# An attention and MoE kernel on one core: value preparation placed between a batch's first scores and its first x, and the last block's last step tile by tile

## The chip, the core and the metric

The kernel runs on one core of one Trainium2 chip. A core has a matrix engine (PE, whose weight loads are listed apart as PEld), three engines for elementwise work (DVE, ACT, POOL) and SP, which here only issues DMAs. Each engine runs its own stream of instructions in order and waits for the others by semaphores. Matmuls write to PSUM, which has eight banks of 128 × 512 float32; SBUF is the working memory.

The metric is the device time of one execution in microseconds. It is told as the median of several runs; a profile shows one execution.

## The reference

Eight batches of 576 tokens and eight heads of 64 columns go through attention over pooled keys and values, and the result, as 4608 tokens of 512 columns, through a gated MLP with 2048 hidden columns.

```python
k_p = k.reshape(B, H, 72, 8, D).mean(axis=3)      # keys and values pooled by 8
v_p = v.reshape(B, H, 72, 8, D).mean(axis=3)
scores = q @ k_p.T / sqrt(D)
attn = softmax(scores)
x = attn @ v_p                                     # (4608, 512), heads side by side
h = x @ w_in
g = h * clip(h + 3, 0, 6) / 6
out = g @ w_out
```

All of it is in float32. The kernel splits an operand into a high and a low part (float32r) and adds three products, high by high, high by low and low by high.

## The kernel before

**Blocks.** The tokens are cut into ten blocks (`BLOCKS`, L22): 512, 256, 384, six of 512 and 384. For each block the MLP runs in 16 steps, one for each group of 128 hidden columns (`Step`, L761). A step makes `h` (12 matmuls at L774, into one of two PSUM banks), then `relu` on ACT (L782), `gate` on DVE (L786), `hi` on ACT (L790) and `lo` on DVE (L794). Two steps later its `out` adds three matmuls for each tile of 128 tokens (L803) into the tile's own PSUM bank. After the 16th step ACT scales the tile (L806) and SP stores it (L808).

**Attention under the MLP.** While block j runs its MLP, the attention of block j + 1 is made between its pieces. "Block j's run" below is that stretch. The attention is a list of steps (`block_steps`, L609): a scores step for a tile and half of the heads (matmuls L412, maximum on DVE L416, exponentials on ACT L420, division on POOL L448 and L454), a transposes step (L518 and L520 on PE, then L529 and L540 on ACT, L530 and L541 on DVE, which empty the PSUM bank), and an x step (`av`, L578: the products with the values at L583 and a copy by ACT at L585). `Paced` spreads the list evenly over the slots of the MLP: one in each `h`, one before each tile of an `out`. At the end of a run `split_x` (L556) makes the next block's x into its two parts.

**Side steps.** A batch's keys and values are prepared from batch 2 on by side steps (`side_steps`, L592): four loads of keys (L200) and four sums by eight on DVE (L214) with two scalings on ACT each (L222); six loads of values (L228, and L233 in three DMAs each) and six sums on DVE (L332), after the fourth and the last of which ACT and DVE write the values' parts (L345, L346, L359, L360). `plan()` (L970) attaches each side step to an attention step, which it goes ahead of. Loads, the sums of values (`vsum`), the second half of a q tile that spans two batches and the outputs share a ring of four SBUF buffers (`ring`, L131). The prepared keys and values have two buffers each, by turns of the batches.

**Order.** Up to the third step of block 1's run, the order of each engine's instructions is written out by hand (`ORDER`, L32; the numbers count an engine's instructions in program order), and `put_in_order` (L141) fixes it. Behind it the framework lays the instructions out, by program order and by what a simulated timeline finds ready.

Of the kernel before, what the change touches and what calls it, by code (L numbers as in the profile page):

```python
# [8 lines left out]
F32 = mybir.dt.float32  # L9
# [8 lines left out]
P = 128  # L18
# [3 lines left out]
BLOCKS = [512, 256, 384] + [512] * 6 + [384]  # L22
# [1 line left out]

TLAG = 3

SIDE = 20

WSCALE = 2.0**8

# [28 lines left out]
        93 62 90 85 87 94 117-120 91 126-129 99 102 92 115 103 100 112 136 65 130 137 101 138-139 116 113 124  # L59
        121 114 125 122 140 123 143 66 63 131 64 132 134 144 135 153 133 145 141 147 142 150 148 146 154 151 149  # L60
        155 157 160 156 152 166 158 161 159 167 170-172 162-163 168 164 173 165 174 176 178 169 175 183 177
        180-181 179 187 186 184 188 185 194-197 189 202-205 198-199 182 200 208-211 190-191 201 206-207 192
        212-213 193
    """,
    "Pool": """
# [1 line left out]
    """,  # L67
    "SP": """
        2-3 1 0 4-5 8 6-7 14 9 11 10 22-24 21 20 13 12 15 18 16 19 25-26 28 31 17 27 32 34 33 29 41 30 44 51 35
        48 46 43 36 47 39 52 59 42 37-38 45 40 50 49 53-55 57-58 60-62 64 63 56  # L70
    """,
}

# [2 lines left out]
def attention_moe_kernel(  # L76
# [19 lines left out]
    nc = tc.nc  # L96
    NB, _, NPAIR, S = q.shape
    SP = S // POOL
    NT, DM = out.shape
    NF = w_in.shape[0]  # L100
# [7 lines left out]
    starts = [sum(BLOCKS[:j]) for j in range(len(BLOCKS))]  # L108

    parts_of = []  # L110
    for j, t in enumerate(starts):
        end, mine = t + BLOCKS[j], []
        while t < end:
            n = min(end, (t // S + 1) * S, t + (256 if j == 0 else end)) - t
# [14 lines left out]
    psum = ctx.enter_context(tc.tile_pool(name="psum", bufs=1, space=PSUM))  # L129

    def ring(name):  # L131
        return pool.tile([P, S], F32, name=name, tag="ring", bufs=4)

    def behind(ins, name):
        no_sync = mybir.DependencyInfo(mybir.DependencyClass.NoSync, mybir.DependencyReason.DATA)
        tc.add_manual_dep(ins, name, no_sync, reason="order")

    traced = nc.cur_bb.bb.instructions
# [59 lines left out]
    def load_k(b, p):  # L198
        kraw[b, p] = ring("kst")
        nc.sync.dma_start(kraw[b, p], k[b, p])  # L200
# [3 lines left out]
    def prep_k(b, p):  # L204

        two = b == 0
        if not two:
            ks = pool.tile([P, 1, SP], F32, name="ksum", bufs=1)
        elif p % 2 == 0:
            ks = ksum[p // 2] = piece(0, 2 * SP).rearrange("p (i s) -> p i s", i=2)  # L210
        else:
            ks = ksum[p // 2]
        i = p % 2 if two else 0
        nc.vector.tensor_reduce(  # L214
            out=ks[:, i], in_=kraw.pop((b, p)).rearrange("p (s o) -> p s o", o=POOL), axis=AX.X, op=ALU.add
        )
        if i == two:

            scale = 1.0 / (POOL * D**0.5)
            for h in range(2):  # L220
                rows = slice(h * D, (h + 1) * D)
                nc.scalar.mul(kbds[b % 2][rows, p - i : p + 1, h * SP : (h + 1) * SP], ks[rows], scale)  # L222
# [3 lines left out]
    def load_v(b, p):  # L226
        vraw[b, p] = ring("vst")
        nc.sync.dma_start(vraw[b, p][:, : POOL * D], v[b, p])  # L228

    def load_vr(b, g):  # L230
        vraw[b, NPAIR + g] = ring("vst")
        for c in range(3):
            nc.sync.dma_start(vraw[b, NPAIR + g][c * REM : (c + 1) * REM, : POOL * D], vr[b, g])  # L233
# [88 lines left out]
    def prep_v(b, p):  # L322


        if p == 0:
            if b not in W:
                place_v(b)
            sums = ring("vsum")[:, : (NPAIR + NG) * D]
            vsum[b] = sums.rearrange("p (c d) -> p c d", d=D)
        n = P if p < NPAIR else 3 * REM  # L330
        vs, st = vsum[b], vraw.pop((b, p))
        nc.vector.tensor_reduce(  # L332
            out=vs[:n, p], in_=st[:n, : POOL * D].rearrange("p (o d) -> p d o", o=POOL), axis=AX.X, op=ALU.add
        )
        if p == NPAIR - 1:
            place_heads(b, vs[:, :NPAIR])
        elif p == NPAIR + NG - 1:
            place_rest(b, vs[:, NPAIR:])
# [253 lines left out]
    def side_steps(b):  # L592

        ks = [lambda p=p: load_k(b, p) for p in range(NPAIR)]
        ks += [lambda p=p: prep_k(b, p) for p in range(NPAIR)]
        vs = []
        n = NPAIR + NG
        for p in range(n + 2):
            if p < n:
                vs.append(lambda p=p: load_v(b, p) if p < NPAIR else load_vr(b, p - NPAIR))  # L600
            if p >= 2:
                vs.append(lambda p=p: prep_v(b, p - 2))
        return ks, vs
# [31 lines left out]
    w_in_hi, w_in_lo, w_out_hi, w_out_lo = {}, {}, {}, {}  # L635
# [113 lines left out]
    class Block:  # L749
        def __init__(self, j, banks):  # L750
            self.j, self.nt, self.banks, self.pos = j, BLOCKS[j] // P, banks, {}

        def sums(self, t):
            if t not in self.pos:
                self.pos[t] = psum.tile([P, DM], F32, name="pso", tag=self.banks[t])
            return self.pos[t]

    def no_slot():
# [2 lines left out]
    class Step:  # L761
# [33 lines left out]

        def out(self, slot=no_slot):
            f, blk = self.f, self.blk
            for t in range(self.t0, self.t1):
                slot()
                pos = blk.sums(t)  # L800
                ghi, glo = (x[:, (t - self.t0) * P : (t - self.t0 + 1) * P] for x in (self.ghi, self.glo))
                for i, (l, r) in enumerate(((ghi, w_out_hi), (ghi, w_out_lo), (glo, w_out_hi))):
                    nc.tensor.matmul(pos, l, r[f], start=f == 0 and i == 0, stop=f == NF - 1 and i == 2)  # L803
                if f == NF - 1:
                    o = ring("o")[:, :DM]
                    nc.scalar.mul(o, pos, 1.0 / WSCALE**2)  # L806
                    at = starts[blk.j] + t * P
                    nc.sync.dma_start(out[at : at + P, :], o)  # L808


    ident = const.tile([P, P], F32, name="ident")
# [10 lines left out]
    class Paced:  # L822
# [5 lines left out]
        def slot(self):  # L828
            self.at += 1
            self.upto(min(len(self.steps), -(-len(self.steps) * self.at // self.n)))  # L830
# [61 lines left out]
    b = [Scores(t, g) for g in range(NG) for t in B]  # L892
# [77 lines left out]
    def plan():  # L970


        every = []
        for j in range(2, len(BLOCKS)):
            later_steps[j] = block_steps(j)
            every += later_steps[j]
        for b in range(2, NB):
            ends = [n for n, x in enumerate(every) if x[2] and b - 2 in x[3]]
            begin = max(ends) + 1 if ends else 0
            end = min(n for n, x in enumerate(every) if x[2] == "scores" and b in x[3])  # L980
            begin = max(begin, end - SIDE)
            ks, vs = side_steps(b)
            for n, x in enumerate(ks + vs):
                every[begin + n * (end - begin) // len(ks + vs)][0].append(x)

    plan()

    def run(steps, lag, attention, first_slot=0, preps={}):
# [41 lines left out]
    for j in range(1, len(BLOCKS)):  # L1030
        blk = Block(j, ["o0", "o1", "o2", "o3"])
# [45 lines left out]
```

## Time and profile before

| | us |
|---|---|
| median of 3 runs (lowest, highest) | 928.81 (928.56, 930.24) |
| the profiled execution's own time | 929.94 |
| span of the profiled execution, first to last instruction | 928.2 |
| PE busy | 910.8 |
| DVE busy | 456.0 |
| ACT busy | 460.3 |
| POOL busy | 78.0 |

Busy times are shares of the span. A matmul is recorded from its start to a modelled end, and the next one starts before that end, so the distance between two starts is shorter than one record. A row of the timeline gives the start, the duration, engine, line, operation and the count of instructions merged into it; in square brackets stands the idle time of the engine before it and what ended that. A row of the table by stretches gives the stretch, its length, then busy time and count of PE, PEld, DVE, ACT and POOL, the granted clock of PE as a fraction of full speed, the DMA share and GB/s.

### The profile page before, as it was taken

The numbers are of one execution on the slowest core, as the hardware profiler recorded it, in microseconds if no ns is written. First come the engines' busy times: TensorE is split into PE (matmuls) and PEld (weight loads), VectorE is DVE, ScalarE is ACT, GpSimd is POOL, SyncE is SP. The second block draws the span as 40 slices with busy tenths as digits, with TensorE's granted clock in tenths as the row PEclk, the third lists the DMA queues.
The fourth block names the chain that finished last, engine by engine and source line by source line (L and its number), as shares of the span: only waits on it lengthen the run. The fifth ranks groups of instructions, "written<-read, shape, count | busy, mean of one in ns | idle before, by whom it ended". The sixth has DMA issues, their size and how long they took to land.

```text
span 928.2 us, 12551 instructions
## 1 busy us (share of the span) xinstructions
PE 910.8 (98%) x4500; PEld 775.8 (84%) x4500; DVE 456.0 (49%) x915; ACT 460.3 (50%) x1340; POOL 78.0 (8%) x167
## 2 busy tenths in 40 slices
PE   7899998999999999999999999999999999999997
PEld 7788887999887888888888888888888888888996
DVE  6999846564358532744354325733454224332321
ACT  5998665574446534544364435533544244333322
POOL 4100001021001100101011100110011001000000
PEclk9999999999999999999999999999999999999999
DMA  9960205040015000400050003200200000000100
GB/s 306 392 242 3 89 12 171 25 124 18 1 41 159 12 12 32 151 12 6 1 168 15 12 1 115 78 12 1 74 24 12 1 34 25 0 1 7 40 1 34
DMA packets 41790, 57.17 MB, mean 62 GB/s; under 512 B 7552, under 2 KB 23424, under 8 KB 41728
## 3 DMA queue, kind: packets, MB, share of 16 engines
q1 hardware_dynamic: 41584, 56.37, 18.9%
q8 instruction: 35, 0.57, 0.3%
q14 instruction: 27, 0.22, 0.1%
q10 hardware_dynamic: 144, 0.00, 0.0%
HBM read 46.93 MB, written 9.44 MB: 61 GB/s over the span
## 4 chain that ended last, share of the span: by engine, by line
PE 91%; DVE 3%; DMA 3%; ACT 1%; issue 1%; SPq 1%; ACTq 0%; DVEq 0%
PE psh L774 41%; PE pso L803 41%; PE psa L583 4%; PE psa L412 4%; PE psa L518 1%; DMA kst<-k_l 1%; DVE vsum L332 1%; DMA stage<-v_l 1%; PE psa L290 1%; DMA vst<-v_l 1%; DVE ksum L214 0%; PE psa L520 0%; DVE mx L416 0%; ACT o L806 0%; DMA out<-o 0%
## 5 line engine op out<-in xcount | busy, mean ns | idle before, releaser
L774 PE MATMUL psh<-xhi,w 128*128 128x512 f32 (+2 forms) x1288 | 403.3, 373 | 0.2
L803 PE MATMUL pso<-w,ghi 128*128 128x512 f32 x1152 | 363.5, 397 | 0.0
L774 PEld LDWEIGHTS psh<-xhi,w 128*128 128x128 f32 x1288 | 238.3, 189 | 37.3 <-DVE g L786 0.7
L803 PEld LDWEIGHTS pso<-w,ghi 128*128 128x128 f32 x1152 | 209.7, 188 | 36.2
L774 PE MATMUL psh<-xlo,w 128*128 128x512 f32 (+2 forms) x644 | 237.7, 369 | 0.0
L786 DVE SCALAR_TENSOR_TENSOR g<-g,psh 128x512 f32<-128x512 f32 (+2 forms) x161 | 101.4, 630 | 272.2 <-ACT g L782 271.6
L803 PE MATMUL pso<-w,glo 128*128 128x512 f32 x576 | 223.0, 393 | 0.5 <-DVE glo L794 0.5
L782 ACT ACTIVATE g<-psh,small 128x512 f32<-128x512 f32 (+2 forms) x161 | 103.7, 644 | 218.1 <-PE psh L774 204.3
L774 PEld LDWEIGHTS psh<-xlo,w 128*128 128x128 f32 x644 | 121.6, 189 | 18.6
L794 DVE TENSOR_TENSOR glo<-g,ghi 128x512 fp32r<-128x512 f32 (+2 forms) x161 | 103.4, 642 | 60.2 <-ACT ghi L790 59.0
L790 ACT CAST ghi<-g 128x512 fp32r<-128x512 f32 (+2 forms) x161 | 92.9, 577 | 76.3 <-DVE g L786 72.7
L803 PEld LDWEIGHTS pso<-w,glo 128*128 128x128 f32 x576 | 108.1, 188 | 23.3 <-DVE glo L794 0.9
L420 ACT ACTIVATE e<-psa,mx 128x72 f32<-128x72 f32 x256 | 78.5, 321 | 45.9 <-DVE mx L416 45.0
L448 POOL TENSOR_TENSOR a<-e,sm 128x256 f32<-128x256 f32 x60 | 38.1, 635 | 508.8 <-DVE sm L437 232.4
L420 ACT ACTIVATION_READ_ACCUMULATOR e<-psa,mx 128x1 f32 x256 | 52.6, 205 | 0.0
L412 PEld LDWEIGHTS psa<-kbd,qt 128*128 128x128 f32 x288 | 43.6, 191 | 4.4 <-issue 0.2
L416 DVE TENSOR_REDUCE mx<-psa 128x4 f32<-128x288 f32 x72 | 32.5, 454 | 29.2 <-PE psa L412 28.8
L412 PE MATMUL psa<-kbd,qt 128*128 128x144 f32 x288 | 46.0, 287 | 0.0
L332 DVE TENSOR_REDUCE vsum<-vst 128x64 f32<-128x512 f32 (+1 forms) x36 | 37.7, 1065 | 6.0 <-DMA vst<-vr_l 2.6
L585 ACT COPY x<-psa 128x192 f32<-128x192 f32 (+7 forms) x60 | 22.9, 387 | 31.7 <-PE psa L583 31.4
L529 ACT CAST ahi<-psa 128x256 fp32r<-128x256 f32 (+1 forms) x70 | 24.4, 350 | 25.1 <-PE psa L518 12.7
L530 DVE TENSOR_TENSOR alo<-psa,ahi 128x256 fp32r<-128x256 f32 (+1 forms) x70 | 27.4, 393 | 17.4 <-ACT ahi L529 16.7
(92 smaller groups left out, 611.4 us busy)
## 6 DMA issues: line engine op xcount, KB each, us to landing
out<-o SPq DMA_DIRECT2D x36, 256.0 KB, 2.3
raw<-w_in_l SPq DMA_DIRECT2D x16, 512.0 KB, 8.5
raw<-w_out_l SPq DMA_DIRECT2D x16, 512.0 KB, 9.2
kst<-k_l SPq DMA_DIRECT2D x28, 288.0 KB, 3.9
qt<-q_l SPq DMA_DIRECT2D x28, 256.0 KB, 3.3
vst<-v_l SPq DMA_DIRECT2D x24, 256.0 KB, 3.1
vst<-vr_l SPq DMA_DIRECT2D x36, 64.0 KB, 2.0
stage<-k_l SPq DMA_DIRECT2D x4, 288.0 KB, 3.7
```

Of the source, the lines that this page charges most:

```text
L332: nc.vector.tensor_reduce(out=vs[:n, p], in_=st[:n, : POOL * D].rearrange("p (o d) -> p d o", o=POOL), axis=AX.X, op=ALU.add)
L412: nc.tensor.matmul(to, qt[:, p, :], kbds[b % 2][:, p, :], start=r == 0, stop=r == last)
L416: nc.vector.tensor_reduce(out=self.mx, in_=self.ps, axis=AX.X, op=ALU.max, negate=True)
L420: nc.scalar.activation(self.e[:, h], self.ps[:, h], AF.Exp, bias=self.mx[:, h : h + 1], accum_out=self.sm[:, h : h + 1])
L448: engine.tensor_tensor(out=self.a[:, : 4 * D].rearrange("p (h s) -> p h s", h=4), in0=e[:, :, :D], in1=sm[:, :, None].broadcast_to([P, 4, D]),
L583: nc.tensor.matmul(ps, l, r, start=n == 0, stop=n == len(mms) - 1)
L774: nc.tensor.matmul(self.ps, l[f][:, c, :], r[:, c, :], start=c == 0 and i == 0, stop=c == NCC - 1 and i == 2)
L782: nc.scalar.activation(self.g, self.ps, AF.Relu, bias=half, scale=1.0 / (6.0 * WSCALE))
L786: nc.vector.scalar_tensor_tensor(out=g, in0=g, scalar=1.0, in1=self.ps, op0=ALU.min, op1=ALU.mult)
L790: nc.scalar.copy(self.ghi, self.g)
L794: nc.vector.tensor_tensor(out=self.glo, in0=self.g, in1=self.ghi.bitcast(F32), op=ALU.subtract)
L803: nc.tensor.matmul(pos, l, r[f], start=f == 0 and i == 0, stop=f == NF - 1 and i == 2)
```

## The change

The plan of the side steps is changed. Before, all 20 side steps of a batch were spread over at most `SIDE` = 20 attention steps that end with the batch's first scores step, and not before the last use of the batch two back. Now the eight steps for the keys are spread over at most `SIDE` = 12 attention steps that end with the first scores step, and the twelve for the values over the attention steps from the first scores step to the batch's first x step; each begins no earlier than the same kind of use by the batch two back ends. The value steps of a batch thereby stand one run later. Four key loads leave the part of SP's order that is written by hand, and ACT's list has one instruction (207) moved behind another (192).

In the last block the third and last tile is summed in two halves of 256 columns, each in a PSUM bank of its own, through all 16 steps. Its halves are scaled by ACT and by DVE and stored by two DMAs. The matmuls of that block's last `out` are held in program order: tile by tile, and half by half in the last tile.

```diff
-SIDE = 20
+SIDE = 12
...
     "Activation":
-        180-181 179 187 186 184 188 185 194-197 189 202-205 198-199 182 200 208-211 190-191 201 206-207 192
+        180-181 179 187 186 184 188 185 194-197 189 202-205 198-199 182 200 208-211 190-191 201 206 192 207
...
     "SP":
-        48 46 43 36 47 39 52 59 42 37-38 45 40 50 49 53-55 57-58 60-62 64 63 56
+        48 46 43 36 47 39 52 59 42 37-38 45 40 50 49 53-55 57-58 60 56
...
         def sums(self, t):
             if t not in self.pos:
-                self.pos[t] = psum.tile([P, DM], F32, name="pso", tag=self.banks[t])
+                banks = [self.banks[t]]
+                if self.j == len(BLOCKS) - 1 and t == self.nt - 1:
+                    banks.append(self.banks[t + 1])
+                n = DM // len(banks)
+                self.pos[t] = [
+                    (slice(i * n, (i + 1) * n), psum.tile([P, DM], F32, name="pso", tag=b)[:, :n])
+                    for i, b in enumerate(banks)
+                ]
             return self.pos[t]
...
         def out(self, slot=no_slot):
             f, blk = self.f, self.blk
+            mark = len(traced)
             for t in range(self.t0, self.t1):
                 slot()
-                pos = blk.sums(t)
                 ghi, glo = (x[:, (t - self.t0) * P : (t - self.t0 + 1) * P] for x in (self.ghi, self.glo))
-                for i, (l, r) in enumerate(((ghi, w_out_hi), (ghi, w_out_lo), (glo, w_out_hi))):
-                    nc.tensor.matmul(pos, l, r[f], start=f == 0 and i == 0, stop=f == NF - 1 and i == 2)
-                if f == NF - 1:
-                    o = ring("o")[:, :DM]
-                    nc.scalar.mul(o, pos, 1.0 / WSCALE**2)
-                    at = starts[blk.j] + t * P
-                    nc.sync.dma_start(out[at : at + P, :], o)
+                products = (ghi, w_out_hi[f]), (ghi, w_out_lo[f]), (glo, w_out_hi[f])
+                for cols, pos in blk.sums(t):
+                    for i, (l, r) in enumerate(products):
+                        nc.tensor.matmul(pos, l, r[:, cols], start=f == 0 and i == 0, stop=f == NF - 1 and i == 2)
+                if f < NF - 1:
+                    continue
+                o = ring("o")[:, :DM]
+                at = starts[blk.j] + t * P
+                for (cols, pos), scaled in zip(blk.sums(t), (nc.scalar.mul, nc.vector.tensor_scalar_mul)):
+                    scaled(o[:, cols], pos, 1.0 / WSCALE**2)
+                    nc.sync.dma_start(out[at : at + P, cols], o[:, cols])
+            if f == NF - 1 and blk.j == len(BLOCKS) - 1:
+                mine = [i for i in traced[mark:] if i.engine == mybir.EngineType.PE]
+                for x, y in zip(mine, mine[1:]):
+                    behind(y, x.name)
...
     def plan():
...
+        def uses(kind, b):
+            return [n for n, x in enumerate(every) if x[2] == kind and b in x[3]]
+
         for b in range(2, NB):
-            ends = [n for n, x in enumerate(every) if x[2] and b - 2 in x[3]]
-            begin = max(ends) + 1 if ends else 0
-            end = min(n for n, x in enumerate(every) if x[2] == "scores" and b in x[3])
-            begin = max(begin, end - SIDE)
-            ks, vs = side_steps(b)
-            for n, x in enumerate(ks + vs):
-                every[begin + n * (end - begin) // len(ks + vs)][0].append(x)
+            begin = uses("scores", b)[0]
+            for side, kind, begin, end in zip(
+                side_steps(b), ("scores", "av"), (begin - SIDE, begin), (begin, uses("av", b)[0])
+            ):
+                begin = max([begin] + [n + 1 for n in uses(kind, b - 2)])
+                for n, x in enumerate(side):
+                    every[begin + n * (end - begin) // len(side)][0].append(x)
```

## The prediction

> **What bounds the kernel now.** The order of reading: the page's busy times, the waits of PE, the chain of waits around the longest wait, then the timeline and the table by stretches of that place.
>
> ```profile
> PE 910.8 (98%) x4500; PEld 775.8 (84%) x4500; DVE 456.0 (49%) x915; ACT 460.3 (50%) x1340; POOL 78.0 (8%) x167
> ```
>
> PE is busy for 910.8 of 928.2 us, so 17.4 us are all that a reordering can win, and some of that is the start and the end. The waits of PE (engine, line, awaited; us in all, times, longest) say which part lies in reach:
>
> ```profile
> PE psa L518 <- DVE arem L541: 2.4, 1, 2.4
> ...
> PE psa L583 <- DVE arem L541: 0.6, 1, 0.6
> PE pso L803 <- DVE glo L794: 0.5, 1, 0.5
> ```
>
> These three come after the first 100 us. The long one is in block 1's run (the MoE of block 1, under which the attention for block 2 is made). The chain there, and DVE's timeline:
>
> ```profile
> 149.57 5.39 DMA vst<-v_l
> ...
> 155.06 1.07 DVE vsum L332
> ```
> ```profile
> 152.30 0.43 DVE L794 TENSOR_TENSOR glo<-g,ghi 128x256 fp32r<-128x256 f32 x1 [0.37 <-ACT ghi L790]
> 155.06 1.07 DVE L332 TENSOR_REDUCE vsum<-vst 128x64 f32<-128x512 f32 x1 [2.33 <-DMA vst<-v_l]
> 156.16 0.28 DVE L541 TENSOR_TENSOR arem<-psa,arem 32x128 fp32r<-32x128 f32 x1
> ...
> 158.82 0.29 DVE L541 TENSOR_TENSOR arem<-psa,arem 32x128 fp32r<-32x128 f32 x1
> ```
>
> DVE reaches batch 2's first value sum at 152.73, finds its load of 149.57 not landed, and stands for 2.33 us with everything behind it; then the sums take 1.07 us each, and the second `arem`, which frees a PSUM bank for the next transposes, runs only at 158.82. PE stands from 156.87 to 159.25. What follows is seen in the table by stretches (after POOL's count: granted clock, DMA share, GB/s):
>
> ```profile
> 159.00:160.00 1.00, 0.75 (x5) 0.59 (x6) 0.97 (x3) 0.69 (x3) 0.00 (x0) 1.00 0.56 131
> 160.00:161.00 1.00, 1.00 (x7) 1.00 (x7) 1.00 (x5) 0.38 (x1) 0.00 (x0) 0.53 0.55 160
> 161.00:162.00 1.00, 1.00 (x7) 1.00 (x6) 1.00 (x3) 0.95 (x4) 0.81 (x2) 0.50 0.09 29
> 162.00:163.00 1.00, 1.00 (x7) 1.00 (x6) 0.94 (x3) 0.24 (x1) 0.05 (x1) 0.50 0.00 0
> 163.00:164.00 1.00, 1.00 (x5) 0.81 (x5) 1.00 (x2) 0.41 (x1) 0.00 (x0) 0.77 0.16 31
> ```
>
> Just behind the stall the granted clock is halved for 3.4 us: 0.47 + 0.50 + 0.50 + 0.23 = 1.70 us of work lost, where PE looks fully busy. The stall's place costs 2.38 + 1.70 = 4.08 us.
>
> **The value sums moved: the stall.** With SIDE at 20 all twenty side steps of batch 2 lay on the 16 attention steps of block 2, which is block 1's run: 12 of them values. By the new plan block 1's run keeps the keys alone, loads at steps 4, 5, 7, 8 and sums at 10, 11, 13, 14, and the values go to block 2's run: loads at steps 0, 1, 2, 5, 8, 10, sums at 4, 6, 9, 12, 13, 14, the first x step of batch 2 at 16. The sum that stood at 155.06 isn't in block 1's run any more, so DVE does `arem` at 152.7, and what is late next is nothing seen: the table of PE's waits names no other in that run. I take −2.38 for the wait and −1.70 for the clock. Bounds: 0, if a wait of the same kind comes back with its clock, and −4.08.
>
> On the clock the Trainium skill speaks, against half of this: TensorE: Matmul & The Clock Gate, section "Why this matters for your kernels", asks only that no idle gap exceed about 3 us, and this gap of 2.38 us is shorter. If that holds, the slow stretch has another cause and stays; the sum would keep the 1.70. The same page's window of 3413 ns agrees with the 3.4 us measured at 0.50. I go by the row: the slow stretch starts 0.8 us after the stall ends, and after 100 us none comes without one.
>
> **The same edit in block 3's run.** Batch 3's values were meant for block 2's run too, but the sums come only here:
>
> ```profile
> 213.64 58.90 SPq L193 DMA_DIRECT2D qt<-q_l  x3
> ```
> ```profile
> 272.20 3.02 DVE L332 TENSOR_REDUCE vsum<-vst 128x64 f32<-128x512 f32 x3 [0.62 <-PE psa L412]
> ```
> ```profile
> 289.88 0.96 PE L803 MATMUL pso<-w,glo 128*128 128x512 f32 x3 [0.51 <-DVE glo L794]
> ```
> ```profile
> 299.46 0.30 PE L583 MATMUL psa<-arem,vrem 96*128 96x64 f32 x1 [0.58 <-DVE arem L541]
> ```
>
> The ring has four buffers; loads, `vsum`, the second half of a tile that spans two batches, and the outputs share it. The q load of the tile across batches 2 and 3 holds one from step 9 of block 2's run until block 4's first scores, and three value loads hold the rest, so `vsum` had none. Batches 3 and 4 were then summed back to back, and PE waited 0.51 + 0.58 us. The new plan spreads batch 3 over 20 steps and starts batch 4's keys only at step 14 of block 3's run. I take −1.09; bounds 0 (other DVE-bound waits of this size instead) and −1.4, as a 512-column matmul is recorded for 0.385 us and followed after 0.2275 (rows of the last block, below), so that idle time is understated by 0.16 at each of the two.
>
> What the moved work costs where it lands: per batch six sums, two `vlo`, four `vrem` on DVE, and on ACT two `vhi`, four `vrem`.
>
> ```profile
> L332 DVE TENSOR_REDUCE vsum<-vst 128x64 f32<-128x512 f32 x24 | 24.9, 1064 | 3.2 <-DMA vst<-v_l 2.5 <-PE psa L412 0.6
> L360 DVE SCALAR_TENSOR_TENSOR vrem<-vsum,small,vrem 32x128 fp32r<-32x128 f32 x24 | 6.8, 336 | 0.2
> L346 DVE SCALAR_TENSOR_TENSOR vlo<-vsum,vhi 64x256 fp32r<-64x256 f32 x12 | 5.1, 423 | 1.9 <-POOL vlo L318 1.7
> L359 ACT ACTIVATE vrem<-vsum,small 96x128 fp32r<-96x128 f32 x24 | 7.7, 392 | 4.5 <-DVE vsum L332 4.5
> ```
> ```profile
> 183.00:258.00 75.00, 75.00 (x400) 68.34 (x399) 33.72 (x80) 38.79 (x132) 8.88 (x20) 1.00 0.15 44
> ```
>
> DVE: 6 × 1.06 + 2 × 0.42 + 4 × 0.34 = 8.6 us, into a run where it is busy 33.7 of 75 us. It hides behind PE as long as no sum stands before a piece that frees a bank. The six values' DMAs (four, and two of three pieces) and the keys' four queue on SP behind the q loads; an SP issue takes some 0.44 us (1.32 for three, below), and none waits at the head in front of work that PE needs within a step. For what DVE's new sums delay by the way I add +0.3 (bounds 0 and +1.1, the two waits above). The order written out by hand loses four SP loads (the key loads of batch 2) and lets ACT's third output of block 0 go before a `ghi`:
>
> ```profile
> 138.76 0.41 ACT L790 CAST ghi<-g 128x256 fp32r<-128x256 f32 x1 [2.44 <-PE pso L803]
> 139.07 0.59 ACT L806 ACTIVATE o<-pso 128x512 f32<-128x512 f32 x1
> ```
>
> ACT idles 2.44 us there, so this is 0; without that cover `ghi` would come 0.6 us later.
>
> **The deadline that is now closer.** Batch 2's last sum is at step 14, with the third tile's transposes, and its products' first use two steps on. Before, that place was:
>
> ```profile
> 235.92 0.38 PE L518 MATMUL psa<-ident,a 128*128 128x128 f32 x2
> ...
> 242.23 0.39 PE L583 MATMUL psa<-ahi,vhi 128*128 128x512 f32 x1
> ...
> 258.43 0.63 PE L803 MATMUL pso<-w,ghi 128*128 128x512 f32 x2
> ```
>
> From 235.9 the sum (1.1) and the four pairs on ACT and DVE (4 × 0.39 + 0.34) end by 239, 3 us ahead of 242.2. The ring makes it tighter: at steps 8 and 9 two key loads of batch 3 and the q load stand ahead of the last value load, which then waits for the first key sum at 14: its DMA (2.0 us to land, below) and the rest put the end near 243. PE has its own steps to do meanwhile, so I cost this at 0.
>
> ```profile
> vst<-vr_l SPq DMA_DIRECT2D x36, 64.0 KB, 2.0
> out<-o SPq DMA_DIRECT2D x36, 256.0 KB, 2.3
> ```
>
> **The last block.** For its third tile each of the 16 steps issues six products of 256 columns for three of 512.
>
> ```profile
> 164.75 1.44 PE psh L774 x12
> ```
> ```profile
> 336.23 2.73 PE psh L774 x12
> 912.96 2.08 PE pso L803 x9
> 917.14 5.72 PE pso L803 x25
> ```
>
> 256 columns come every 0.120 us, 512 every 0.2275 (2.73 / 12) or, in this block, 0.231. So 48 × (0.240 − 0.231 to 0.2275) = +0.43 to +0.60; I take 0.5. By the cycle table of the same page (section "Back-to-back issue gap") a cut costs 6 cycles, which would be an estimated 0.12 us in all; the rows decide. The end:
>
> ```profile
> 922.46 0.84 PE L803 MATMUL pso<-w,glo 128*128 128x512 f32 x3
> 922.89 1.57 ACT L806 ACTIVATE o<-pso 128x512 f32<-128x512 f32 x3 [3.99 <-PE pso L803]
> 923.51 1.32 SPq L808 DMA_DIRECT2D out<-o  x3
> ```
>
> Today all three tiles finish together and ACT scales them one after the other until 924.46; the last issue ends at 924.83. Tile by tile the first is ready at about 922.5 and the second at 923.1; the halves end at about 923.45 and 923.8, the last goes through DVE (0.41 for 256 columns out of PSUM, the `gate` row's kind) until 924.2. SP is then the limit: four issues of 0.37 (the last of today's, from 924.46 to 924.83), from 923.1, each behind its output, end between 924.6 and 924.9. The last transfer carries 128 KB, so lands 0.1 to 0.3 sooner (between the 2.0 and 2.3 above). With the 0.5 in it, the end moves by −0.4 to +0.1; I take −0.1.
>
> ```profile
> L589 DVE TENSOR_TENSOR xlo<-psa,xhi 128x256 fp32r<-128x256 f32 x8 | 3.2, 409 | 0.0
> ```
>
> **Sum.** The profiled execution took 929.94 us (span 928.20 and 1.74 around it): −2.38 − 1.70 − 1.09 + 0.30 − 0.10 = −4.97, so 924.97. The runs shown have a median of 928.81 and go from 928.56 to 930.24; that spread is the size of the 1.70, so runs near the median may lack the slow stretch. The new kernel would lack it in any case, so I forecast 925.0 as its median too.
>
> **The rivals.**
> 1. The slow stretch stays (the page's reading above): 925.0 + 1.7 = 926.7. For it: a gap under 3 us. Against: it follows the only long gap.
> 2. The stall moves. Block 2's run gets a sum at the head of DVE whose load hasn't landed, at steps 4 to 6, behind six value and q loads that SP issues at the run's start; bank-freeing work waits, and the same 4.1 come back: 929.1. For it: landing took 5.39 us where loads came in a burst. Against: the loads are now one or two steps (some 4 us each, 75 us for 20) apart, two ahead of their sums.
> 3. The plan isn't what runs: the ring decides, as it did with batch 3's sums (planned from step 11, done at 272). Then only block 1's run is relieved: 929.94 − 4.08 + 0.30 − 0.10 = 926.1.
> 4. Slower. The ring starves batch 2's last value load until block 2's run is over, say until a key sum behind x's splitting:
>
> ```profile
> 259.75 2.50 DVE L562 TENSOR_TENSOR xlo<-x,xhi 128x512 fp32r<-128x512 f32 x4
> ```
>
> That ends at 262.25; load 3.3 (three issues of 0.44 and 2.0), sum 1.1, `vrem` 1.9 make values ready at 268.5, and four groups of four matmuls (3.7), a copy of 0.5 (as an output's scaling, 1.57 for three) and the first split (0.63 on each of ACT and DVE, 2.50 for four) give block 3 its x at 274.0. PE's work from 258.43 is nine tiles of 0.69, until 264.6: 9.4 us standing and 1.7 of half clock, 929.94 − 4.97 + 11.1 = 936.1. It decides once the values come later than 264.6 − 5.5 = 259.1, against the 243 above: 16 us of room speak against it. For it: today's case 3.
>
> **How the numbers follow.** Forecast 0.62, rival 1 0.10, 2 0.16, 3 0.05, 4 0.07. About 0.2% (1.9 us) is what a measurement can tell from no change, so faster means below 926.95: forecast, 1 and 3, 0.77; rival 2 is the same, 0.16; 4 is slower. Behind the part ordered by hand the order of all engines is laid out anew; for that I allow 1.1 us either way, the size of the two small waits. The forecast's own range then goes from 925.0 − 0.3 (−1.4 for −1.09) − 0.3 (no new small waits) − 0.3 (the better end) − 1.1 = 923.0 to 925.0 + 0.8 (+1.1 for +0.3) + 0.2 (the worse end) + 1.1 = 927.1. For 8 in 10 it reaches up to rival 2, 929.1, and leaves out rival 4 and what lies between the two.
>
> **What would show it.** Right: no wait of PE over 1 us after 100 us, the granted clock 1.00 from 150 to 170, block 1's run 4 us shorter, batch 2's sums between 195 and 240, batch 3's between 260 and 330, four last issues of which the last ends about where it did. Wrong: a granted clock of 0.5 anywhere after 100 us, a wait of PE for `arem`, `vrem` or x in block 2's or 3's run, or blocks 4 to 8 changing by more than 0.3 us each, since nothing there stands still today.

## The result and the profile after

| | before | after |
|---|---|---|
| median of 4 runs each on one chip (lowest, highest), us | 928.68 (927.67, 930.24) | 922.57 (921.59, 924.38) |
| ratio, with its 95% interval | | 0.993 (0.9911 to 0.9949) |
| the profiled execution's own time, us | 929.94 | 923.03 |
| its span, us | 928.2 | 921.2 |

The change makes the kernel faster by 6.1 us in the medians and by 6.91 us in the profiled pair. The forecast was 925.0, a gain of 3.8 against the median then known (928.81), with a range down to 923.0: the direction was right, the size was not, and the time lies 0.43 us below the range.

One execution of the first experiment below, the profiled one (5214 us), and one of the kernel before on the same chip (1007 us) were disturbed; the medians given there hold them (without them 923.1 and 929.8), the ratios don't.

The busy times of the page after, and the head of its list of PE's waits (engine, line, awaited; us in all, times, longest):

```profile
PE 908.1 (99%) x4548; PEld 776.8 (84%) x4548; DVE 457.4 (50%) x916; ACT 461.7 (50%) x1340; POOL 82.0 (9%) x167
```
```profile
PE idle L270 <- POOL ident masks.py:199: 2.4, 1, 2.4
```

PE issues 48 matmuls more (the halves) and is nevertheless busy for 2.7 us less. Every wait that the list names lies in the first 100 us; the 2.4 us for `arem` in block 1's run and the 0.6 and 0.5 us in block 3's are gone. The place of the stall in DVE's timeline after, and in the table by stretches:

```profile
153.72 0.74 DVE L214 TENSOR_REDUCE ksum<-kst 128x72 f32<-128x576 f32 x1
...
155.52 0.28 DVE L541 TENSOR_TENSOR arem<-psa,arem 32x128 fp32r<-32x128 f32 x1
156.10 0.42 DVE L794 SCALAR_TENSOR_TENSOR g<-g,psh 128x256 f32<-128x256 f32 x1 [0.30 <-ACT g L790]
156.55 0.29 DVE L541 TENSOR_TENSOR arem<-psa,arem 32x128 fp32r<-32x128 f32 x1
```
```profile
160.00:161.00 1.00, 1.00 (x7) 0.83 (x6) 0.73 (x3) 0.47 (x1) 0.28 (x1) 1.00 0.00 0
```

A key sum of 0.74 us stands where the value sum had waited for its load. The two `arem` come 1.03 us apart, where they had been 2.66 apart. The clock stays at 1.00 in this stretch of 1 us and in those around it.

To see where the time went, the span is cut at the same five matmuls in each kernel: the first `h` of block 1's run, of block 3's, of block 4's and of block 9's, then the last matmul and the end of the span. Blocks 1 and 2's runs are taken together, since a different order of the attention's pieces moves work over the line between them. First the kernel before, then after (the count behind PE's busy time is of the merged records):

```profile
124.50:263.44 138.94, 136.53 (x774) 123.64 (x772) 71.37 (x169) 74.39 (x251) 15.84 (x34) 0.99 0.20 59
263.44:364.30 100.86, 99.54 (x470) 81.95 (x469) 53.95 (x108) 47.59 (x151) 8.48 (x18) 1.00 0.18 51
364.30:853.50 489.20, 489.20 (x2329) 409.06 (x2327) 208.10 (x426) 218.39 (x666) 41.05 (x86) 1.00 0.12 37
853.50:922.92 69.42, 69.42 (x349) 62.73 (x347) 17.80 (x32) 19.62 (x37) 0.00 (x0) 1.00 0.04 16
922.92:928.15 5.23, 0.39 (x2) 0.00 (x0) 0.00 (x0) 1.54 (x3) 0.00 (x0) 0.99 0.41 152
```
```profile
125.32:259.56 134.24, 134.24 (x773) 122.02 (x772) 71.08 (x169) 74.62 (x251) 16.74 (x34) 1.00 0.18 55
259.56:358.03 98.47, 98.47 (x470) 82.33 (x469) 46.40 (x96) 46.24 (x145) 8.55 (x18) 1.00 0.16 46
358.03:847.40 489.37, 489.37 (x2328) 409.09 (x2327) 216.25 (x438) 220.95 (x672) 43.93 (x86) 1.00 0.13 40
847.40:917.22 69.82, 69.82 (x397) 65.07 (x395) 17.82 (x32) 20.60 (x38) 0.00 (x0) 1.00 0.04 16
917.22:921.25 4.03, 0.28 (x3) 0.07 (x1) 0.42 (x1) 0.48 (x2) 0.00 (x0) 1.00 0.55 197
```

| stretch | difference, us |
|---|---|
| start, to block 1's run | +0.82 |
| blocks 1 and 2 | −4.70 |
| block 3 | −2.39 |
| blocks 4 to 8 | +0.17 |
| block 9 to its last matmul | +0.40 |
| last matmul to the end | −1.20 |
| span | −6.90 |

After, PE has no idle time left from the first cut to the last matmul: every length equals its busy time. Block 3's run holds more than its waits had shown: PE's 470 records there fill 99.54 us before and 98.47 after, for the same work. Of the 2.39 us, 1.32 was idle time and 1.07 stood as busy time. The trace of before has four idle gaps in this run, two of them too short for its list of waits: 0.13, 0.51, 0.58 and 0.11 us. At each of them the 0.16 is lost too by which a record is longer than the distance to the next one. That makes an estimated 0.6 of the 1.07; the rest must lie in delays too short to show as gaps.

The sums of values after, by DVE's timeline (line 332, first and last of each batch):

```profile
191.25 1.06 DVE L332 TENSOR_REDUCE vsum<-vst 128x64 f32<-128x512 f32 x1
...
203.25 1.07 DVE L332 TENSOR_REDUCE vsum<-vst 96x64 f32<-96x512 f32 x1 [0.17 <-DMA vst<-vr_l]
268.90 1.09 DVE L332 TENSOR_REDUCE vsum<-vst 128x64 f32<-128x512 f32 x1
...
277.79 1.06 DVE L332 TENSOR_REDUCE vsum<-vst 96x64 f32<-96x512 f32 x1
367.32 1.07 DVE L332 TENSOR_REDUCE vsum<-vst 128x64 f32<-128x512 f32 x1 [0.40 <-DMA vst<-v_l]
```

Batch 2's sums are through by 204.3. Batch 3's are nearly as bunched as before (268.9 to 278.9; before 272.2 to 280.6). Batch 4's, which before were a second bunch in block 3's run (294.3 to 302.5), start in block 4's run. The end after:

```profile
916.76 0.33 SPq L820 DMA_DIRECT2D out<-o  x1
917.45 0.33 SPq L820 DMA_DIRECT2D out<-o  x1
917.53 0.42 DVE L819 TENSOR_SCALAR o<-pso 128x256 f32<-128x256 f32 x1 [3.98 <-PE pso L813]
917.87 0.41 SPq L820 DMA_DIRECT2D out<-o  x1
918.40 0.38 SPq L820 DMA_DIRECT2D out<-o  x1
```

The scaling ends 0.73 us after the last matmul starts (917.95 − 917.22), where it had been 1.54 (924.46 − 922.92). SP issues the first store before the last matmul starts and the other three almost back to back; the fourth starts 0.45 us after its scaling ended, behind the third.

### The profile page after: what moved, and what is told of

Its sections match the earlier page's. It is cut to its first block, busy times and chain, and to the rows that moved or that the text cites. A ratio compares the mean times of both kernels' runs of the same rounds, so it can differ in the third digit from the quotient of the medians.

```text
span 921.2 us, 12671 instructions
## 1 busy us (share of the span) xinstructions
PE 908.1 (99%) x4548; PEld 776.8 (84%) x4548; DVE 457.4 (50%) x916; ACT 461.7 (50%) x1340; POOL 82.0 (9%) x167
## 4 chain that ended last, share of the span: by engine, by line
PE 96%; DVE 2%; DMA 1%; SPq 0%; ACT 0%; issue 0%; DVEq 0%
PE pso L813 43%; PE psh L782 43%; PE psa L583 4%; PE psa L412 4%; PE psa L518 2%; DMA kst<-k_l 1%; PE psa L520 0%; DVE u L689 0%; ACT stage L420 0%; DVE u L700 0%; SPq L257 0%; DVE stage L448 0%; SPq L259 0%; DVE a L510 0%; SPq L262 0%
## 5 line engine op out<-in xcount | busy, mean ns | idle before, releaser
L813 PE MATMUL pso<-w,ghi 128*128 128x512 f32 (+1 forms) x1184 | 367.0, 391 | 0.0
L813 PEld LDWEIGHTS pso<-w,ghi 128*128 128x128 f32 x1184 | 214.1, 188 | 36.0
L813 PE MATMUL pso<-w,glo 128*128 128x512 f32 (+1 forms) x592 | 225.9, 386 | 0.0
L813 PEld LDWEIGHTS pso<-w,glo 128*128 128x128 f32 x592 | 111.1, 188 | 21.7
L448 POOL TENSOR_TENSOR a<-e,sm 128x256 f32<-128x256 f32 x60 | 41.2, 687 | 517.2 <-PE pso L813 180.3
L436 DVE TENSOR_SCALAR sm<-sm 128x4 f32<-128x4 f32 x72 | 12.4, 176 | 48.7 <-ACT e L420 45.7
```

The lines of the kernel that those rows point to most:

```text
L448: engine.tensor_tensor(out=self.a[:, : 4 * D].rearrange("p (h s) -> p h s", h=4), in0=e[:, :, :D], in1=sm[:, :, None].broadcast_to([P, 4, D]),
L813: nc.tensor.matmul(pos, l, r[:, cols], start=f == 0 and i == 0, stop=f == NF - 1 and i == 2)
```

## The experiments

The theory: the plan alone makes the gain, by three separate things in blocks 1 to 3 (the stall, its slow stretch, and DVE's crowding in block 3's run); the last block's edit is worth nothing that can be told. The rivals: that the end is part of the gain; that the stall left for another reason than the sum's waiting load; that block 3's time hangs on batch 2's move. Each experiment's stretches are cut as above. The time of before that stands beside each is from runs on the same chip.

**Plan alone.** The change with `sums` and `out` of before.

```diff
-                for cols, pos in blk.sums(t):
-                    for i, (l, r) in enumerate(products):
-                        nc.tensor.matmul(pos, l, r[:, cols], start=f == 0 and i == 0, stop=f == NF - 1 and i == 2)
+                for i, (l, r) in enumerate(((ghi, w_out_hi), (ghi, w_out_lo), (glo, w_out_hi))):
+                    nc.tensor.matmul(pos, l, r[f], start=f == 0 and i == 0, stop=f == NF - 1 and i == 2)
...
```

> The new plan of side steps and the new order by hand, with the last block as before. By the split of the two spans (block 1's run 4.7 us shorter, block 3's run 2.4, the last block and its stores 0.8) it should stand at 922.6 + 0.8 = 923.4 us, PE with no wait over 0.5 us after 100 us and no half clock there. The prediction's own terms (4.1 for the stall and its clock, 0.8 for block 3's run) would give 923.8 or more against 928.7, that is 924.0. If the last block's edit were the larger part, it would stand above 925.

Measured: 923.34 against 929.9, ratio 0.9935 (0.9922 to 0.9949). The same kernel was profiled again:

> The new plan with the last block as before, once more, for its profile. Blocks 1 and 2's runs 134.3 together, block 3's 98.47, blocks 4 to 8 489.4, block 9 to its last matmul 69.42 (no halves), and from the last matmul to the end 4.8 to 5.2 as in the kernels with that end; the whole near 923.3. If the halves and the order of the last step were worth anything, it would be over 923.5 and its last part over 74.5.

Measured: 922.81 in the one execution, against 930.47. Blocks 1 and 2 took 134.25, block 3 98.46, as after; the last block as before:

```profile
846.78:916.20 69.42, 69.42 (x349) 62.73 (x347) 17.80 (x32) 19.62 (x37) 0.00 (x0) 1.00 0.04 16
916.20:921.03 4.83, 0.38 (x2) 0.00 (x0) 0.00 (x0) 1.54 (x3) 0.00 (x0) 0.93 0.44 165
```

So the plan alone gives the whole gain, as far as these runs can tell.

**Last block alone.** The kernel before with the new `sums` and `out`.

```diff
+                if self.j == len(BLOCKS) - 1 and t == self.nt - 1:
+                    banks.append(self.banks[t + 1])
...
+            if f == NF - 1 and blk.j == len(BLOCKS) - 1:
+                mine = [i for i in traced[mark:] if i.engine == mybir.EngineType.PE]
+                for x, y in zip(mine, mine[1:]):
+                    behind(y, x.name)
```

> The last block as after, the plan as before: the stall of 2.4 us near 157 and the half clock behind it stay. Theory (the last stores are limited by the DMA engines, so that it counts when the first store starts): from the last matmul's start to the end of the span 4.0 us as after, not 5.2 as before, in all 0.8 us less than before, 927.9. Rival (the prediction: SP's four issues limit the end): 928.3 to 928.8.

Measured: 930.02 against 929.9, ratio 1.0 (0.9988 to 1.0012). The last two rows:

```profile
855.43:925.27 69.84, 69.84 (x397) 65.13 (x395) 17.83 (x32) 20.58 (x38) 0.00 (x0) 1.00 0.04 16
925.27:929.61 4.34, 0.28 (x3) 0.07 (x1) 0.42 (x1) 0.48 (x2) 0.00 (x0) 0.90 0.51 183
```

The halves cost 0.42 us and the end wins it back: it takes 4.34 us here, and 4.03 in the profile of the change with the same last block. This profile also holds something that nobody had asked for. The stall is there, and no slow stretch behind it (PE's wait, then the stretches of 1 us at that place and the whole of blocks 1 and 2):

```profile
PE psa L518 <- DVE arem L541: 2.4, 1, 2.4
```
```profile
162.00:163.00 1.00, 1.00 (x10) 1.00 (x10) 1.00 (x3) 0.36 (x2) 0.00 (x0) 1.00 0.51 135
...
165.00:166.00 1.00, 0.87 (x6) 0.49 (x5) 0.97 (x3) 0.41 (x1) 0.00 (x0) 1.00 0.83 216
```
```profile
126.95:265.03 138.08, 135.23 (x774) 121.96 (x772) 71.40 (x169) 74.25 (x251) 15.86 (x34) 1.00 0.20 59
```

Without the slow stretch these runs still take 138.08 us, 0.86 less than in the profile with it. PE is busy for 1.30 us less and idle for 0.44 more. DVE is busy from 0.95 to 1.00 in every stretch from 159 to 168, and PE, at full clock, waits again (0.87 busy above). That fits a PE that catches up with DVE; it is one profile.

**Order alone.** The last step tile by tile, without the halves.

```diff
-                if self.j == len(BLOCKS) - 1 and t == self.nt - 1:
-                    banks.append(self.banks[t + 1])
```

(in the kernel of the last experiment)

> The kernel before, with only the order of the last step changed: tile by tile, the third tile whole, so without the 48 further matmuls and the fourth store. Theory (the end is the DMA engines' 2.1 us for three tiles, counted from the first store): the first store starts 1.1 us earlier against the last matmul, the third tile is scaled by ACT in 0.6 us and its 256 KB then still have to go, 0.7 us, so the end comes 0.6 to 1.0 us earlier than before: 927.7 to 928.1. Rival (the halves make the gain): 928.6.

Measured: 928.27 against 930.83, ratio 0.9978 (0.9966 to 0.9989).

```profile
852.36:921.80 69.44, 69.44 (x348) 62.76 (x347) 17.80 (x32) 20.45 (x38) 0.00 (x0) 1.00 0.04 16
921.80:926.15 4.35, 0.39 (x2) 0.00 (x0) 0.00 (x0) 0.94 (x2) 0.00 (x0) 0.82 0.49 183
```

The last block takes 73.79 us from its first `h` to the end; halves and order together took 74.18 and, in the change, 73.85; the end of before 74.65 and 74.25. So the order saves some 0.5 to 0.9 us, and the halves give back 0.06 to 0.39 of it. The 2.6 us between the medians are not in the profile, which shows those 0.5 to 0.9. In part they go with the clock: 11 of this chip's 17 runs of before had a mean granted clock of 0.996, and 2 of these 12. Among the runs at 0.998 the means lie 1.4 us apart, among those at 0.996 0.7.

**Batch 2 as before.** The new plan for batches 3 to 7 only, and the last block as before.

```diff
+            if b == 2:
+                ks, vs = side_steps(b)
+                for n, x in enumerate(ks + vs):
+                    every[n * begin // len(ks + vs)][0].append(x)
+                continue
```

> Batch 2's side steps where they were before, those of batches 3 to 7 by the new plan, the last block as before. Theory (two separate gains): the stall near 157 stays with its half clock, block 3's run is 2.4 us shorter than before: 928.7 - 2.4 = 926.3. By the prediction's sizes for block 3's run (0.8 net): 927.9. If the gain in block 3's run hung on batch 2's values being out of the way, it would be 928.7.

Measured: 927.99 against 929.9, ratio 0.9978 (0.9968 to 0.9987).

```profile
126.23:264.65 138.42, 136.27 (x774) 123.57 (x772) 70.91 (x169) 74.56 (x251) 15.56 (x34) 0.99 0.18 53
264.65:363.11 98.46, 98.46 (x470) 82.40 (x469) 46.49 (x96) 46.26 (x145) 8.53 (x18) 1.00 0.16 46
```

The stall and its slow stretch are back, and block 3's run has its full gain. So block 3's gain doesn't hang on batch 2.

**Sums later.** The kernel before, with its loads where they were, and batch 2's six value sums three attention steps later and each held behind the DVE instruction ahead of it in the program, so that both `arem` come first.

```diff
+            sums = [x for n, x in enumerate(vs) if n in (2, 4, 6, 8, 10, 11)]
             for n, x in enumerate(ks + vs):
-                every[begin + n * (end - begin) // len(ks + vs)][0].append(x)
+                at = begin + n * (end - begin) // len(ks + vs)
+                every[min(at + 3, end - 1) if b == 2 and x in sums else at][0].append(x)
...
+        if ahead:
+            behind(traced[-1], ahead)
```

> The kernel before, with batch 2's six value sums three attention steps later and held in program order on DVE, so that both pieces that free the PSUM banks go ahead of the first sum; loads where they were, all of it still in block 1's run. Theory (PE stood because DVE waited for a load in front of those pieces, not because block 1's run holds too much work): the wait of 2.4 us and the half clock behind it go, 928.7 - 4.1 = 924.6, perhaps 0.5 more for other small waits. Rival (too much DVE work for the short run): 1 to 2 us of waits stay in block 1's run, 926 to 927.

Measured: 926.22 against 929.9, ratio 0.9958 (0.9945 to 0.9972). DVE's timeline (lines stand three lower in this kernel), then the stretches:

```profile
154.96 0.29 DVE L544 TENSOR_TENSOR arem<-psa,arem 32x128 fp32r<-32x128 f32 x1 [0.33 <-ACT arem L543]
...
157.87 1.09 DVE L333 TENSOR_REDUCE vsum<-vst 128x64 f32<-128x512 f32 x1
```
```profile
126.27:260.69 134.42, 134.42 (x773) 122.06 (x772) 71.60 (x169) 74.41 (x251) 15.79 (x34) 1.00 0.20 61
260.69:361.28 100.59, 99.56 (x471) 82.06 (x469) 53.87 (x108) 47.54 (x151) 8.48 (x18) 1.00 0.18 52
```

All the sums, their loads and DVE's work are still in block 1's run (DVE busy 71.60 there and in block 2's, against 71.37), and the stall, the slow stretch and 4.5 us are gone. What cost the time was one waiting sum that stood ahead of the `arem`, not the load on DVE or on the queue. Block 3's run keeps its old length, as it should.

**Batches 3 and 4 apart.** The kernel before with the new plan for batches 4 to 7 alone, and with it for batch 3 alone.

```diff
         for b in range(2, NB):
+            if b in (2, 3):
+                ends = [n for n, x in enumerate(every) if x[2] and b - 2 in x[3]]
+                begin = max(ends) + 1 if ends else 0
...
+                continue
```

Batches in that list are planned as before, with 20 for `SIDE`; the second kernel has (2, 4, 5, 6, 7) there.

> The kernel before with the new plan for batches 4 to 7 alone; batches 2 and 3 and the last block as before. It asks which part of the plan shortened block 3's run from 100.86 to 98.47 us. If it is batch 3's value sums, which the ring holds back until that run, the run stays at 100.6 to 100.9. If it is batch 4's twenty side steps, bunched on that run's last thirteen attention steps, it falls to 98.5. If only both together overload DVE, it is near 99.5. Blocks 1 and 2's runs stay at 138.4 to 138.9, the whole between 928 and 930.

> The kernel before with the new plan for batch 3 alone; batches 2 and 4 to 7 and the last block as before. If batch 3's late value sums are what block 3's run lost its 2.4 us to, it falls to 98.5 though batch 4 stays bunched, and the whole is near 928. If batch 4's bunch is, it stays at 100.6 to 100.9. If both together are, it may even grow, since batch 3's spread values now share the run with batch 4's keys and values; then 101 or more.

Measured: 929.03 and 928.70 against 930.47, ratios 0.9986 (0.9977 to 0.9996) and 0.9982 (0.9972 to 0.9993). Block 3's run, first with batches 4 to 7 by the new plan, then with batch 3 by it, and the first sums of values in the first:

```profile
263.02:362.05 99.03, 98.90 (x471) 82.19 (x469) 46.27 (x96) 45.88 (x145) 8.48 (x18) 1.00 0.13 38
```
```profile
265.19:365.33 100.14, 99.03 (x471) 82.15 (x469) 53.84 (x108) 48.09 (x151) 8.06 (x18) 1.00 0.20 60
```
```profile
271.78 3.02 DVE L332 TENSOR_REDUCE vsum<-vst 128x64 f32<-128x512 f32 x3 [0.62 <-PE psa L412]
```

Four profiles with the old plan for both (before, the last block alone, the order alone, the sums later) have 100.86, 101.15, 100.26 and 100.59 here. With batch 4 moved the run takes 99.03, 1.2 to 2.1 less, though batch 3's sums still begin at 271.8 and three of them run back to back. With batch 3 moved it takes 100.14, barely under the four, and both batches' sums stay in the run. PE's waits agree: with batch 4 moved both waits of before are gone; with batch 3 moved PE still waits twice (0.8 and 0.3 us, until 298.0 and 301.0), among and just behind batch 4's sums (292.5 to 300.3). DVE's timeline before, at the two waits, shows what stood there:

```profile
288.47 0.75 DVE L214 TENSOR_REDUCE ksum<-kst 128x72 f32<-128x576 f32 x1 [3.31 <-DMA kst<-k_l]
289.14 0.68 DVE L794 TENSOR_TENSOR glo<-g,ghi 128x512 fp32r<-128x512 f32 x1
...
298.12 1.04 DVE L332 TENSOR_REDUCE vsum<-vst 128x64 f32<-128x512 f32 x1
299.19 0.22 DVE L541 TENSOR_TENSOR arem<-psa,arem 32x64 fp32r<-32x64 f32 x1
```

The first wait is a small copy of block 1's stall: DVE stood for 3.31 us before batch 4's first key sum, whose load hadn't landed, with the `glo` that PE needed behind it. The second is an `arem` behind one of batch 4's value sums. So by these profiles, one of each kernel, the larger part of block 3's gain came from batch 4's leaving that run (DVE's busy time there falls from 53.9 to 46.3), and the full 98.47 needs both. The medians can't tell the two kernels apart: they gained 1.4 and 1.8 us, and the intervals of their ratios overlap.

**The end.** Three kernels on the change: without the store of the last block's first tile (its 128 rows of the output are not written); with the last two steps' `out` made tile by tile; and that without the halves.

```diff
+                    if blk.j < len(BLOCKS) - 1 or t > 0:
                         nc.sync.dma_start(out[at : at + P, cols], o[:, cols])
```
```diff
+            if u == len(steps) + lag - 2 and steps[0].blk.j == len(BLOCKS) - 1:
+                for n in range(steps[0].t1):
+                    for x in steps[-2:]:
+                        x.out(slot, [n])
...
+                break
```

> The kernel after, without the store of the last block's first tile (128 rows of the output are not written). Theory (DMA throughput, 768 KB in 2.1 us): 256 KB less, so the end comes up to 0.7 us earlier against the last matmul: 3.3 to 3.6 us from the last matmul's start to the end of the span instead of 4.0. Rival (SP's issues or the last half's scaling limit): 4.0 unchanged, or 3.7 if the fourth issue moves up by one issue of 0.35.

> The kernel after, with the last two steps' outputs tile by tile instead of the last one's, halves kept. The first tile is complete 1.4 us earlier against the last matmul and the second 0.7. Theory (the end counts from the first store): stores no longer queue up, the end is set by the last half alone, 3.3 to 3.5 us from the last matmul's start to the end of the span, 922.6 - 0.6 = 922.0. Rival (the last half's scaling and issue already set the end): no change, 922.6.

> As the run with the last two steps tile by tile, but the third tile whole: 48 matmuls and one store fewer. PE ends 0.3 to 0.5 us earlier (the halves' price, 0.39 between the two profiles), the last tile is scaled in 0.6 instead of 0.42 and its store carries 256 KB, 0.35 us longer. Theory: about even with the halves, 921.9 to 922.2; if the prediction's price of the halves (0.5) holds and the end is set by issue and scaling, 0.3 us better than them.

Measured: 922.56, 922.78 and 923.01 against 930.83, ratios 0.9915 (0.9897 to 0.9933), 0.9916 (0.9899 to 0.9933) and 0.9919 (0.9902 to 0.9937). The last row of each:

```profile
916.02:919.93 3.91, 0.28 (x3) 0.08 (x1) 0.42 (x1) 0.48 (x2) 0.00 (x0) 1.00 0.39 136
```
```profile
917.52:921.09 3.57, 0.28 (x3) 0.08 (x1) 0.42 (x1) 0.35 (x1) 0.00 (x0) 1.00 0.43 149
```
```profile
916.91:920.81 3.90, 0.38 (x2) 0.00 (x0) 0.00 (x0) 0.60 (x1) 0.00 (x0) 0.90 0.36 137
```

The first was to show that what the queue has to move at the end sets the end. A store of 256 KB less moved it by 0.12 us (4.03 to 3.91): that idea falls. It doesn't refute the forecast's word that SP is the limit there: the store left out had been issued before the last matmul started, and the other three issues stand as in the change. Two steps tile by tile end 0.46 us earlier (3.57). There the third issue is out of the way and the fourth starts 0.83 us after the last matmul does, where it had been 1.18 (918.40 − 917.22):

```profile
918.35 0.38 SPq L819 DMA_DIRECT2D out<-o  x1
```

That is 0.35 of the 0.46 and speaks for SP as the limit. It isn't shown, since two profiles of one and the same end differ by 0.31 (4.03 and 4.34). Without the halves, two steps tile by tile lose as much at the end (3.90) as the shorter last block gives (69.42 against 69.80): 73.37 and 73.32 us together. None of the three differs from the change in its median by an amount that these runs can tell. What remains after the last scaling, 2.8 to 3.3 us in the three kernels with halves, was not taken apart further.

## Why the prediction was right or wrong

**The stall: the mechanism right.** The wait of 2.38 us left with the value sum, as forecast, and moving the sums alone behind the `arem` takes it away as well (134.42 against 134.24). Blocks 1 and 2 gained 4.70 us where the forecast had −2.38 − 1.70 + 0.30 = −3.78, and −4.08 as the bound. The +0.30 for new small waits didn't come: PE doesn't wait at all in those runs after. The rest, 0.6 us, is of the size by which this stretch differs between kernels with the same plan there: 138.42 to 138.94 with the stall and its slow stretch, and 134.24 to 135.36 with the new plan, where the slowest has one wait of 0.5 us for `g`.

**The slow stretch: right here, but not its price everywhere.** Six kernels had the stall and were profiled. In five the clock was halved just behind it, in one it was not; none of the six kernels without the stall shows a halved clock there. So the stretch followed the stall, but not always. The Trainium skill's rule (TensorE: Matmul & The Clock Gate, "Why this matters for your kernels"), no gap over about 3 us, would have left the clock at full speed after 2.1 to 2.4 us; five traces of six speak against it. The price by halved work, 1.70, was too much as a gain of its own: the one profile without the stretch is only 0.3 to 0.9 us shorter than the five with it, probably because DVE, behind by its own stall, sets the pace there. By the same profile the stall alone cost 138.08 − 134.24 = 3.84 us, where the forecast had 2.38. One of the two terms was too small and the other too large; that their sum came near was in part luck.

**Block 3's run: the step that failed.** "The same edit in block 3's run" was put at −1.09 with −1.4 as its bound; it measured −2.39. This miss of 1.30 us is the largest of three that go the same way (0.92 in blocks 1 and 2, 0.70 at the end). Alone it would have left the time inside the range (925.0 − 1.30 = 923.7); without it the time would have been inside too (922.57 + 1.30 = 923.87). Two things were wrong in the step. The size was read from two idle gaps, and PE lost more than that: there were four gaps (1.32 us), and 1.07 of the 2.39 us stood in the profile as busy. The correction of 0.16 for each named wait covered 0.3 of that. And the mechanism was only half right: "the new plan spreads batch 3 over 20 steps" didn't happen. Batch 3's sums stay bunched within 10 us. By the profiles, what relieved DVE was chiefly that batch 4's second bunch went to the next run, where it costs next to nothing (blocks 4 to 8 took +0.17 us together). The forecast named both moves and didn't divide the gain between them; it showed batch 3's late sums (272.20), while the two waits that it counted, up to 289.88 and 299.46, stood behind a key sum and a value sum of batch 4.

**The last block: right within what these runs can tell.** The halves cost 0.40 us (forecast 0.5, bounds 0.43 and 0.60, so just under the lower one). The cycle table of the Trainium skill's page (TensorE: Matmul & The Clock Gate, "Back-to-back issue gap") gave an estimated 0.12; the four kernels with the halves show 69.80 to 69.84 against 69.42 to 69.45, so the rows were the better guide. The end itself moved by −1.20 in the profiled pair, but the same last block as before ended 4.81 to 5.24 us after its last matmul in five other profiles, and the new one 4.34 after it in the profile of the last block alone. With the halves' price the edit is worth −0.1 to −0.8, forecast −0.1 (−0.4 to +0.1), and the runs of the edit alone show no difference. That the fourth issue stands behind the third was forecast rightly; the issues took 0.33 to 0.41 us, with 0.09 and 0.12 between the last three.

**The rivals.** None came. The stall didn't move into block 2's run, the plan was obeyed as to the run in which a batch is prepared, and the ring starved nothing: batch 2's last sum ended at 204.3, where the forecast had reckoned with 243 and the deadline with 259. "Batch 2's sums between 195 and 240" was wrong as to the pace: they ran from 191.25 to 204.3, since the layout put them ahead of the steps that the plan gave them (the transposes that the last sum was planned beside came after 230).

**The base.** The sum was made against the profiled 929.94 and its result taken as the new median. The runs of before have a median 1.3 us lower, so the same gain counted from it would have given 928.68 − 4.97 = 923.7, inside the range as well; the profile of after lies 0.5 over its median. By profiles the change gave 6.91 and the forecast 4.97: −0.92 in blocks 1 and 2, −1.30 in block 3 and −0.70 at the end are the missing gain, +0.17 and a start 0.82 us longer are against it. The start isn't the change's: three other kernels with its plan reach that cut at 124.1 to 124.7. The five profiles with a stretch at half clock between 34 and 38 us, that of after among them, reach it at 125.3 to 127.0, the seven others at 124.1 to 125.3.

## What to carry to other kernels

When an engine works through a bunch of side work, count the busy time of the same matmuls with and without the bunch (here 99.54 against 98.47 us for 470 records), and don't take the named waits for the loss: here more than half of it was elsewhere. An instruction that waits for a DMA is dear by what stands behind it on its engine, so put it behind the instructions that free a PSUM bank; that one reordering was worth 4.5 us in the profile and 3.7 in the medians (929.9 to 926.22). Before a bunch is spread, see whether two bunches share a run, and which of them the waits stand behind: by the profiles here moving one of them away was most of the gain.

## What the runs showed of the hardware

- A stall of PE of 2.1 to 2.4 us was followed by 3.4 us at half clock in five profiles, and not in a sixth with the same stall. The granted clocks of all executions fit that. Two such stretches lower an execution's mean clock to 0.996 (2 × 1.70 of 928 us). Of 110 executions of kernels with the stall 54 had 0.996 or less, and 7 had 0.999 or 1.0; of 32 of kernels without it none was under 0.997, and 16 had 0.999 or 1.0 (the two named at the start left out).
- The same stretch comes at the start too, in some executions of one kernel and not in others: the clock was 0.50 from 14 to 16 us in the profile before and from 35 to 37 in the profile after, and four of the twelve profiles have none there. Of the executions of the change's own kernel two had a mean granted clock of 1.0 (921.59 and 922.1 us) and two of 0.998 (923.03 and 924.38). That is a difference of 1.9 us between the means of two and two; in the three kernels of the last experiment it is 1.1 to 1.5. Half of 3.4 is 1.7.
- Two matmuls of 256 columns cost 0.40 us / 48 = 8 ns more than one of 512.
- The time from the last matmul to the end differs by 0.4 us between profiles of the same last block (4.81 to 4.83, or 5.23 to 5.24; with halves and order 4.03 or 4.34), and SP's issues don't say why: in all six profiles of the old end the last of them ends 1.91 to 1.92 us after the last matmul starts.
